# Gated stage of a fused FNet and ReGLU layer: cross parts of the fifth block in seven stacked matmuls, two products copied into further banks

## The chip, the cores and the metric

The kernel runs on one core of one Trainium2 chip. The metric is the time of one execution in microseconds, as the device measures it; times before are the median of 3 runs. Five engines work side by side, each through its own queue in order: TensorE (PE; its weight loads are shown apart as PEld), VectorE (DVE), ScalarE (ACT), GpSimd (POOL) and SyncE (SP). In this kernel SP and POOL mostly issue DMA transfers.

## The reference

```python
xn = layernorm(x)                       # x: 2048 tokens x 640
a, b = xn @ hid_re.T, xn @ hid_im.T     # 640 x 640
y = seq_re @ a - seq_im @ b             # 2048 x 2048
gate, up = xn @ W_gate, xn @ W_up       # 640 x 1728 each
h = where(gate > 0, gate, 0) * up
out = x + y + h @ W_down                # 1728 x 640
```

All of it is in fp32. This document is about the line of `gate` and `up`, and about what stands around it.

## The kernel before, in words

The layer runs in three stages. The first streams the sequence DFT in four chunks of 512 tokens (`NCHUNK`, names B11, B21, T1, T2, B22, T3, T4) and leaves its products in DRAM. The second, the gated stage, computes gate and up. The third multiplies by the hidden DFT and by W_down and adds everything up.

TensorE is used with fp32r operands. To keep fp32 accuracy each operand is split into a high part (rounded to fp32r by ScalarE) and a low part (the rest, by VectorE): `split`, L124 and L125. A product is then three matmuls, `mm3`, L130 to L132: high by high, high by low, low by high.

The gated stage works feature-major. The 640 features are five blocks of 128, the 1728 columns of the weights are 13 blocks of 128 (`NF`) and a rest of 64. Two halves of the tokens (`q` = 1, then 0) of 1024 tokens each give 26 units (`NU`), one call of `gate_up(n)` each; `gate_up_rest` does the 64 columns before the first and after the last unit. A unit computes gate and up for 128 columns and two chunks of 512 tokens. Seen as 2 x 2 blocks (gate and up by the two chunks) the first four feature blocks are multiplied in seven block products in place of eight, after Strassen and Winograd: the weights' sums S1 to S4 and the data's sums T1 to T4 stand beside the plain blocks A11, A12, A22 and B11, B21, B22. The fifth feature block is not part of this scheme; it is multiplied by itself in `block4` (A4 for gate, U4 for up, G4 their difference; data X4).

TensorE writes into PSUM banks of 128 x 512. In a unit the order on TensorE is: A11 into b1, A12 and A4 into b2, S1 and U4 into b4, S2 onto b1, A22 and U4 into b3, G4 and S4 onto b4, S3 onto b1. Between two products onto the same bank, ScalarE copies the bank out: `p1`, `ob`, `u2`, `u3` (`copy`, L121). VectorE adds the parts (`oa`, L907 and L935). `finals` (L871 to L873) of a unit is written into the next unit, after its first product.

The weights of a unit are prepared one unit ahead (class `Weights`): the DMA into `z` on SP (L840), four sums and G4 on VectorE (`sums`, L846 to L850), rounding on ScalarE (`high`), low parts on VectorE (`low`, L860), into one of two tiles `gw`. In unit 0 this stands later in the unit than in the others, since the weights of unit 1 land late.

Further work is hung into the units by lists: `issues` and `urgent` after `finals`, `loads` with the weights ahead, `besides` after the bank b3 has been given its work. It is: the data sets of the other half of the tokens (`token_step` and `token_sets`, units 1 to 9; they leave whole sets in DRAM), loading and splitting them (`next_set`, units 9 to 13 and 24), and the weights of the third stage (`pair_weights`, L1018 to L1021 and L125, one in each of units 13 to 24; `keep` stores it one unit later). PE, DVE, ACT and POOL keep the order in which the code is written (`manual_schedule`); SP's order is made by a planner.

SBUF is given out by pools; the pools of the gated stage take the place of those of the streaming stage, and a transfer into a new tile waits for the users of the old tiles there. `stage` is a pool of two tiles that lives through both.

Of the kernel before, what the change touches and what calls it, by code (L numbers as in the profile page):

```python
# [7 lines left out]
F32 = mybir.dt.float32  # L8
# [4 lines left out]
P = 128  # L13
S, D, F = 2048, 640, 1728
KD = D // P
CH = 512
# [25 lines left out]
A11, A12, A22 = (2 * P * i for i in range(3))  # L42
A4, U4, G4 = (6 * P + P * i for i in range(3))
S1, S2, S3, S4 = (9 * P + 2 * P * i for i in range(4))
NZ = 17 * P
NRAW = 10 * P
# [12 lines left out]
def fnet_reglu_kernel(  # L59
# [25 lines left out]
    get_gw0 = lambda: gw0_p.tile([P, 2, NZ], F32R, name="gw")  # L85
# [10 lines left out]
    halves = dram_p.tile([NSET, P, 2, W2], F32, name="set1")  # L96

# [263 lines left out]
    def token_sets(q, step, place=None, unit=None):  # L361
# [15 lines left out]
        if step < 2:  # L377
# [12 lines left out]
            made = [([make], "a", lambda v: halves[X4][:, v, cs], lambda ap: ap)]  # L390
            keep_whole = lambda: nc.gpsimd.dma_start(sets[X4][:, cs], t["a"])
# [36 lines left out]
        if unit:  # L428
            unit(load, made[0][0], keep_whole)
            return  # L430

        def halve(name):
            src = t[name]
            t["h" + name] = h = work()[:, : src.shape[1]]
            split(h.bitcast(F32R), src.bitcast(F32R), src)

# [6 lines left out]
        return load, made[0][0], halves_of  # L443

# [9 lines left out]
    def s4_part(g):  # L454

        if "s4" not in late:
            late["s4"] = get_gw0().rearrange("p v z -> p (v z)")
# [314 lines left out]

    early_sets, first_sets = list(SETS_A), list(SETS_B)
# [9 lines left out]
    for step in range(2, SET_STEPS):  # L783
# [6 lines left out]
        at(c, "B22", 2 * i + 1, *([halve["mr"]] if i else halve.values()))  # L790

    def phase(c, names):


        for n in names.split():
            if n == "K":
# [19 lines left out]
    phase(NCHUNK - 1, "T10 T11 T12 T13 T20 B220 T21 B221 T22 T23 K K K A A B222 B223 T30 A T31 A T32 A T33 T40 T41 T42 T43 K")  # L816
# [7 lines left out]
    for n, b, side in (("prep", 2, "left"), ("tmp", 1, "left"), ("wr", 1, "left"), ("hob", 2, "left"), ("z", 2, "left"),  # L824
                       ("stage3", 2, "left"), ("sets", 1, "left"), ("gw1", 1, "right")):
        open_pools[n] = ph2.enter_context(tc.tile_pool(name=n, bufs=b, side=side, reuse_waits="tile"))
    pool = open_pools.__getitem__
    stage3 = lambda: pool("stage3").tile([P, W2], F32, name="st")
    get_gw = (get_gw0, lambda: pool("gw1").tile([P, 2, NZ], F32R, name="gw"))
    NU = 2 * NF  # L830
    tt = nc.vector.tensor_tensor
    SUMS = 8 * P

    class Weights:


        def __init__(self, n):
            self.z2 = pool("z").tile([P, 2 * P + NZ], F32, name="z")
            with tc.issue_after(late["dma"]):
                self.ins = nc.sync.dma_start(self.z2[:, :NRAW], wgu[n % NF]).ins  # L840
            self.n, self.z = n, self.z2[:, 2 * P :]

        def sums(self):
            a21, z = self.z2[:, : 2 * P], self.z
            zz = lambda b: z[:, b : b + 2 * P]
# [540 lines left out]
```

## Time and profile before

| | |
|---|---|
| median of 3 runs | 1025.42 us (1024.63 to 1025.64) |
| span of the profiled execution | 1023.0 us; the page gives no time beside it, and the median stands 2.4 above |
| TensorE busy | 1019.0 us, 4524 matmuls |
| VectorE, ScalarE, GpSimd busy | 816.7, 435.0, 123.1 us |
| granted TensorE clock | 1.000 |
| gated units | 404.1 to 722.4 us |

Busy shares are means over the three stages. A row of a view reads: source line, engine, operation, tile written <- tiles read, shape, count, then busy time and mean duration. In a view in order of time a row begins with start and duration in us, and what stands in brackets at its end is the engine's idle time ahead of it and who ended it. Consecutive instructions of an engine overlap a little in these rows.

### The profile page before, as it was taken

The page shows a single profiled execution, that of the slowest core. Times are in us where ns is not written, and L with a number is a line of the kernel's source. Part 1 is how long each engine was busy: PE and PEld are TensorE (multiplying, and loading weights), DVE is VectorE, ACT ScalarE, POOL GpSimd, SP SyncE. Part 2 cuts the span into 40 slices and gives each one's busy share as a digit, 9 for nine tenths or more (in the row PEclk, how much of TensorE's full clock was granted, in tenths as well). Part 3 has the DMA queues.
Part 4 walks back from the last instruction along what each step waited for, and adds up shares of the span by engine and source line. Part 5 has one row for each costly group of instructions (what it writes and reads, how often), then busy time and mean ns, then how long its engine had stood idle before and what let it go on. Part 6 is the DMA issues. An engine that isn't in the chain of part 4 may idle for free.

```text
span 1023.0 us, 12536 instructions
## 1 busy us (share of the span) xinstructions
PE 1019.0 (100%) x4524; PEld 844.3 (83%) x4524; DVE 816.7 (80%) x1102; ACT 435.0 (43%) x554; POOL 123.1 (12%) x193
## 2 busy tenths in 40 slices
PE   9999999999999999999999999999999999999998
PEld 8888888888888888888888888888888888888887
DVE  7957977998989576788878988888686895777983
ACT  5654453443433333433335444444544434544442
POOL 3521001012210001112210000011100000000000
PEclk9999999999999999999999999999999999999999
DMA  8897734958969885555547676674999467896624
GB/s 321 310 299 284 257 127 160 339 196 272 359 235 350 304 320 148 187 191 180 178 145 271 217 251 239 237 271 166 326 399 307 126 237 252 281 322 214 225 95 139
DMA packets 91389, 249.12 MB, mean 244 GB/s; under 512 B 11328, under 2 KB 32384, under 8 KB 88640
## 3 DMA queue, kind: packets, MB, share of 16 engines
q1 hardware_dynamic: 72720, 174.11, 49.8%
q0 software_dynamic: 18176, 73.67, 19.8%
q8 instruction: 35, 0.57, 0.2%
q10 hardware_dynamic: 432, 0.56, 0.1%
q14 instruction: 26, 0.21, 0.1%
HBM read 185.63 MB, written 61.62 MB: 242 GB/s over the span
## 4 chain that ended last, share of the span: by engine, by line
PE 100%; ACT 0%; issue 0%
PE ps L132 31%; PE ps L131 31%; PE ps L130 31%; PE ps L511 3%; PE ps L541 1%; PE ps L1233 1%; PE ps L112 0%; PE ps L1238 0%; PE ps L1248 0%; ACT y L121 0%
## 5 line engine op out<-in xcount | busy, mean ns | idle before, releaser
L124 ACT ACTIVATE cb<-rw 128x1024 fp32r<-128x1024 f32 x83 | 81.6, 988 | 135.1 <-PE ps L132 96.8
L125 DVE TENSOR_TENSOR cb<-rw,cb 128x1024 fp32r<-128x1024 f32 x83 | 93.7, 1131 | 48.3 <-ACT cb L124 48.1
L124 ACT ACTIVATE cb<-raw 128x1024 fp32r<-128x1024 f32 x71 | 75.3, 1060 | 114.5 <-PE ps L132 106.3
L125 DVE TENSOR_TENSOR cb<-raw,cb 128x1024 fp32r<-128x1024 f32 x71 | 86.8, 1223 | 40.3 <-ACT cb L124 39.9
L130 PE MATMUL ps<-cb,wt 128*128 128x512 f32 x270 | 105.0, 389 | 0.0
L131 PE MATMUL ps<-cb,wt 128*128 128x512 f32 x270 | 105.0, 389 | 0.0
L132 PE MATMUL ps<-cb,wt 128*128 128x512 f32 x270 | 105.0, 389 | 0.0
L130 PE MATMUL ps<-xs_early,gw 128*128 128x512 f32 x260 | 101.2, 389 | 0.0
L132 PE MATMUL ps<-xs_early,gw 128*128 128x512 f32 x260 | 101.1, 389 | 0.0
L131 PE MATMUL ps<-xs_early,gw 128*128 128x512 f32 x260 | 101.1, 389 | 0.0
L121 ACT ACTIVATE gw<-z 128x1024 fp32r<-128x1024 f32 (+1 forms) x52 | 57.7, 1110 | 79.3 <-DVE z L850 78.4
L130 PE MATMUL ps<-cb,xs_late 128*128 128x512 f32 x232 | 90.2, 389 | 0.0
L131 PE MATMUL ps<-cb,xs_late 128*128 128x512 f32 x232 | 90.2, 389 | 0.0
L132 PE MATMUL ps<-cb,xs_late 128*128 128x512 f32 x232 | 90.2, 389 | 0.0
L130 PE MATMUL ps<-cb,xs_early 128*128 128x512 f32 x226 | 87.9, 389 | 0.0
L131 PE MATMUL ps<-cb,xs_early 128*128 128x512 f32 x226 | 87.9, 389 | 0.0
L132 PE MATMUL ps<-cb,xs_early 128*128 128x512 f32 x226 | 87.9, 389 | 0.0
L121 ACT ACTIVATE u<-ps 128x512 f32<-128x512 f32 x52 | 31.2, 599 | 89.1 <-PE ps L132 89.1
L860 DVE TENSOR_TENSOR gw<-z,gw 128x1024 fp32r<-128x1024 f32 (+1 forms) x52 | 64.7, 1283 | 1.3 <-ACT gw L121 1.2
L130 PEld LDWEIGHTS ps<-cb,wt 128*128 128x128 f32 x270 | 50.7, 188 | 10.6
L131 PEld LDWEIGHTS ps<-cb,wt 128*128 128x128 f32 x270 | 50.7, 188 | 10.6
L132 PEld LDWEIGHTS ps<-cb,wt 128*128 128x128 f32 x270 | 50.7, 188 | 10.4
(195 smaller groups left out, 2210.1 us busy)
## 6 DMA issues: line engine op xcount, KB each, us to landing
raw<-in_dft SPq DMA_DIRECT2D x94, 512.0 KB, 5.9
z<-in_wgu SPq DMA_DIRECT2D x26, 640.0 KB, 4.5
wd<-wparts SPq DMA_DIRECT2D x30, 512.0 KB, 5.7
wparts<-pw POOLq DMA_DIRECT2D x12, 1152.0 KB, 5.3
hd<-ob POOLq DMA_DIRECT2D x26, 512.0 KB, 2.9
rw<-hd SPq DMA_DIRECT2D x24, 512.0 KB, 7.1
tk<-in_dft SPq DMA_DIRECT2D x16, 512.0 KB, 6.0
set<-r POOLq DMA_DIRECT2D x16, 512.0 KB, 4.2
```

The lines of the kernel that those rows point to most:

```text
L121: return nc.scalar.activation(o, i, AF.Copy)
L124: nc.scalar.activation(hi, src, AF.Copy)
L125: return nc.vector.tensor_tensor(lo, src, hi.bitcast(F32), op=OP.subtract)
L130: nc.tensor.matmul(ps, wh, mh, start=first, stop=False, skip_group_check=more)
L131: nc.tensor.matmul(ps, wh, ml, start=False, stop=False, skip_group_check=more)
L132: nc.tensor.matmul(ps, wl, mh, start=False, stop=last, skip_group_check=more)
L511: start["pe"] = pin([nc.tensor.matmul(E[0, key], xn_part(n * SG + j, d)[v == 1], b[:, int(v == 2), j], start=False, stop=n % NH == NH - 1 ...
L541: pin([nc.tensor.matmul(E[c, key], xn_part(j, d)[v == 1], b[c][0][:, int(v == 2), j], start=j == 0 and v == 0, stop=False)])
L860: tt(self.w[:, 1, cs], self.z[:, cs], self.w[:, 0, cs].bitcast(F32), op=OP.subtract)
L1233: nc.tensor.matmul(B[out], w[:, 0, v, oo : oo + P], b[:, 0, 0], start=False, stop=last and v == 1, skip_group_check=more)
```

## The change

For the fifth block, the two cross parts (high by low and low by high) leave `block4` and enter the seven-product scheme. The block's 128 rows are cut in two halves of 64, which take the place of a row more in the 2 x 2 scheme. For one half, the weights' high part (64 rows) and low part (64 rows) are stacked into one 128-row operand, and against it stand the data's low and high part stacked; so one matmul adds both cross parts. Each of the seven products gets one such matmul (`product`: six and one), and what remains of `block4` is one matmul, high by high (`fifth_product`), four times in a unit.

The host lays the weights out with the half blocks twice (`twice`), so a unit's weights are 14 x 128 columns in place of 10. On the chip the lower 64 rows of them become low parts (`fifth_high` on ScalarE, `fifth_low` on VectorE), the sums S1 to S4 are made over three blocks each, and only the main two blocks of each get a low part. The data's seven stacks are made once for each half of the tokens (`cross_sets`, four subtractions), kept in DRAM (`crossed`) and loaded into SBUF in three pieces a, b, c (`load_cross`).

The order on TensorE is now: A11 into b1, S1 into b4, S2 onto b1, A12 and A4 onto c, S3 onto b1, S4 and A4 onto b4, U4 onto d, A22 and U4 onto b1. ScalarE copies b1 after A11 into bank c, and b4 after S1 into bank d; TensorE adds onto these copies. Gate's first part leaves c through a Relu on ScalarE.

The diff, cut to its core:

```diff
-A11, A12, A22 = (2 * P * i for i in range(3))
...
+S1, S2, S3, S4 = range(4)
+A11, A12, A22 = range(4, 7)
+P3 = 3 * P
+HS, HA, A4, U4, LOWS = 0, 12 * P, 21 * P, 22 * P, 23 * P
...
+    def cross_sets(q, place):
...
+        def load():
+            t["s"], t["t"] = place(), place()
+            for i, r in enumerate((lo, hi)):
+                for rows, v in ((lo, 1), (hi, 0)):
+                    nc.gpsimd.dma_start(t["s"][rows, i * W2 : (i + 1) * W2], fifth[q][r, v])
...
+        return load, [sub(t1, b12, b11), sub(t2, b22, t1), sub(t3, b22, b12), sub(t4, b21, t2)], keep
...
+    CROSS_PLACES = {"a": (XB11, 2), "b": (XT2, 2), "c": (XT3, 3)}
...
+    def load_cross(q, name):
+        i, n = CROSS_PLACES[name]
+        t = open_pools["cx"].tile([P, 3 * CH], F32R, name="cx") if name == "c" else stages[-1].tile([P, W2], F32R, name="st")
...
+        return nc.sync.dma_start(t[:, : n * CH].bitcast(F32), crossed[q][:, i * CH : (i + n) * CH])
...
+    load, subs, keep = cross_sets(1, work_pair)
+    at(NCHUNK - 2, "T4", 2, load)
+    for g, sub in enumerate(subs):
+        at(NCHUNK - 1, "T1", g, sub)
+    at(NCHUNK - 1, "T2", 0, keep)
...
         if unit:
-            unit(load, made[0][0], keep_whole)
+            unit(load, made[0][0] if step > 1 else [lambda: (make(), halve("a"))], keep_whole)
             return
...
+        def fifth_high(self):
...
+            copy(self.rounded, self.own)
+        def fifth_low(self):
+            tt(self.own, self.own, self.rounded.bitcast(F32), op=OP.subtract)
         def sums(self):
...
+            tt(s1, a21, a22, op=OP.add)
+            tt(s2, s1, a11, op=OP.subtract)
+            tt(s3, a11, a21, op=OP.subtract)
+            tt(s4, a12, s2, op=OP.subtract)
+        def high_sums(self, i):
+            cs = slice(i * 2 * P3, (i + 1) * 2 * P3)
+            copy(self.w[:, cs], self.s[:, cs])
+        def high_own(self):
+            copy(self.w[:, HA:LOWS], self.z[:, P3:])
...
     def finals(n):
-        tt(ob[:, c1], ob[:, c1], u3, op=OP.add)
-        tt(ob[:, c0], b3, u3, op=OP.add)
-        nc.vector.scalar_tensor_tensor(ob, oa, 0.0, ob, op0=OP.max, op1=OP.mult)
+        tt(ob[:, c1], d, u3, op=OP.add)
+        nc.vector.scalar_tensor_tensor(ob[:, c1], oa, 0.0, ob[:, c1], op0=OP.max, op1=OP.mult)
+        tt(ob[:, c0], ob[:, c0], b1, op=OP.mult)
```

`gate_up` after the change, from its first product on:

```python
        if ahead and n:
            ahead.fifth_high()
        product(b1, A11, B11, XB11, True, True)
        if n > 0:
            finals(n - 1)
        for f in issues[n]: f()
        for f in urgent[n]: f()
        copy(c, b1)
        if ahead and n:
            ahead.fifth_low()
            ahead.sums()
        product(b4, S1, T1, XT1, True, True)
        copy(d, b4)
        if n == NF - 1:
            load_cross(0, "a")
        product(b1, S2, T2, XT2, last=True)
        if ahead and n:
            ahead.high_sums(0)
        copy(u2, b1)
        product(c, A12, B21, XB21)
        fifth_product(c, A4, 0)
        nc.scalar.activation(ob[:, c0], c, AF.Relu)
        if n == NF - 1:
            load_cross(0, "b")
        def rest_ahead():
            if ahead:
                ahead.high_sums(1); ahead.low_sums(); ahead.high_own()
            for f in loads[n]: f()
        if n:
            rest_ahead()
        product(b1, S3, T3, XT3, last=True)
        copy(u3, b1)
        if ahead and n:
            ahead.low_own()
        product(b4, S4, B22, XB22)
        fifth_product(b4, A4, 1)
        tt(oa, b4, u2, op=OP.add)
        if ahead and not n:
            ahead.fifth_high(); ahead.fifth_low(); ahead.sums(); ahead.high_sums(0)
            rest_ahead()
            ahead.low_own()
        for f in besides[n]: f()
        fifth_product(d, U4, 1)
        product(b1, A22, T4, XT4)
        fifth_product(b1, U4, 0)
        if n == NF - 1:
            load_cross(0, "c")
        held[n] = b1, d, u3, oa, ob
```

Before unit 0, SP loads in the written order the weights of unit 0, the rest's weights, the stacks c and b, and the weights of unit 1; the stack a is loaded at the end of the streaming stage (`load_first_cross`). The stacks of the other half are made in unit 10 (`cross_step`). The sets that `next_set` loads now come straight into their place and are split there, and X4 needs no split any more.

226 lines of the change are left out of this document (132 added, 94 removed).

## The prediction, made before the changed kernel was run

> **What bounds the kernel now.** First the page (span, busy shares, slices, the chain that ended last) and the clock.
>
> ```profile
> span 1023.0 us, 12536 instructions
> PE 1019.0 (100%) x4524; PEld 844.3 (83%) x4524; DVE 816.7 (80%) x1102; ACT 435.0 (43%) x554; POOL 123.1 (12%) x193
> ...
> PE   9999999999999999999999999999999999999998
> ...
> PE 100%; ACT 0%; issue 0%
> ...
> core 0: 1023.0 us, clock 1.000
> PE ps L112 <- PEq L1379: 0.8, 1, 0.8
> ```
>
> TensorE is the chain, from first to last, at full granted clock, and its only wait in the whole trace is 0.8 us before the first matmul. So a matmul removed is time removed, and a wait added to TensorE is time added in full; nothing covers it. The span is 1023.0; the median of the runs is 1025.42, so 2.4 us lie around the profiled span, and I add my sum to 1025.42.
>
> Then the groups by form and the order of time in the gated stage. There every matmul has the same shape.
>
> ```profile
> L130 PE MATMUL ps<-xs_early,gw 128*128 128x512 f32 x260 | 101.2, 389 | 0.0
> L130 PE MATMUL ps<-r,gw 128*128 128x512 f32 x104 | 40.5, 389 | 0.0
> L130 PE MATMUL ps<-sets_b,gw 128*128 128x512 f32 x104 | 40.5, 389 | 0.0
> ...
> 587.75 0.39 PE L130 MATMUL ps<-xs_early,gw 128*128 128x512 f32 x1
> ...
> 588.88 0.39 PE L132 MATMUL ps<-xs_early,gw 128*128 128x512 f32 x1
> ...
> 599.99 0.39 PE L130 MATMUL ps<-xs_early,gw 128*128 128x512 f32 x1
> ```
>
> Each of L130, L131 and L132 has 260 + 104 + 104 = 468 of them: 1404, or 54 in each of 26 units. Unit 15 starts at 587.75 and unit 16 at 599.99: 12.24 us for 54, 0.22667 us each. Times inside a unit below count from its first matmul.
>
> **Gain.** Before, a unit has seven blocks of six matmuls and four fifth blocks of three: 54. After, it has seven products of seven (six and one cross matmul) and four single fifth products: 53. 26 units save 26 x 0.22667 = 5.89 us. All else that I find costs.
>
> **What the other engines must do in time.** The work of VectorE and ScalarE in unit 15, in order of time:
>
> ```profile
> 588.64 0.69 DVE L871 TENSOR_TENSOR ob<-ob,u 128x512 f32<-128x512 f32 x1 [1.10 <-ACT u L121]
> 589.25 0.69 DVE L872 TENSOR_TENSOR ob<-ps,u 128x512 f32<-128x512 f32 x1
> 589.97 1.23 DVE L873 SCALAR_TENSOR_TENSOR ob<-oa,ob 128x1024 f32<-128x1024 f32 x1
> ...
> 595.78 0.42 DVE L1018 TENSOR_TENSOR pw<-pw 128x256 f32<-128x256 f32 x1
> 596.23 0.42 DVE L1019 TENSOR_TENSOR pw<-pw 128x256 f32<-128x256 f32 x1
> 596.58 0.42 DVE L1020 TENSOR_TENSOR pw<-pw 128x256 f32<-128x256 f32 x1
> 596.91 0.42 DVE L1021 TENSOR_TENSOR pw<-pw 128x256 f32<-128x256 f32 x1
> 597.91 0.96 DVE L125 TENSOR_TENSOR pw<-pw 128x768 f32<-128x768 f32 x1 [0.58 <-ACT pw L124]
> 598.83 0.69 DVE L935 TENSOR_TENSOR oa<-ps,u 128x512 f32<-128x512 f32 x1
> ...
> 588.01 0.60 ACT L121 ACTIVATE u<-ps 128x512 f32<-128x512 f32 x1 [2.06 <-PE ps L132]
> 588.50 1.05 ACT L121 ACTIVATE gw<-z 128x1024 fp32r<-128x1024 f32 x1
> 589.45 0.59 ACT L121 ACTIVATE p<-ps 128x512 f32<-128x512 f32 x1
> 592.90 1.17 ACT L121 ACTIVATE gw<-z 128x1152 fp32r<-128x1152 f32 x1 [2.85 <-DVE z L850]
> ```
>
> Both follow the written order of the code, one after another. From these rows: VectorE starts an instruction 0.08 before the end of the one ahead (588.64, 0.69 long, then 589.25), and 0.03 after it where it needs its result (589.25 to 589.97); ScalarE starts 0.10 before the end (588.01, 588.50). The p copy at 589.45 begins 0.57 after the start of the last matmul that it needs (588.88). L935 ends a line of VectorE work without a break from 588.64, but for 0.58 waiting on ScalarE: in this unit VectorE is done at 11.8 of 12.24. The rows for the new shapes:
>
> ```profile
> L125 DVE TENSOR_TENSOR wt<-wr,wt 128x384 fp32r<-128x384 f32 x12 | 6.6, 550 | 0.0
> L554 DVE SCALAR_TENSOR_TENSOR sb<-sb,sa 128x512 f32<-128x512 f32 x8 | 5.5, 682 | 0.0
> 403.54 0.67 DVE L964 TENSOR_TENSOR st<-ps,st 64x512 f32<-64x512 f32 x1
> L124 ACT ACTIVATE wt<-wr 128x768 fp32r<-128x768 f32 x39 | 32.5, 834 | 12.3 <-DMA wr<-wparts 7.7 <-PE ps L132 2.0 <-DMA wr<-in_hid 1.3
> 1016.08 0.37 ACT L121 ACTIVATE ps<-ps 128x256 f32<-128x256 f32 x1 [4.38 <-PE ps L132]
> L963 ACT ACTIVATE st<-ps x4: 596/596/597, 402.3 to 729.4; 64x512 f32<-64x512 f32 x4
> L130 PEld LDWEIGHTS ps<-sets_b,gw 128*128 128x128 f32 x104 | 19.5, 188 | 4.0
> ```
>
> A sum of 384 columns is 0.55, a multiply of 512 with a maximum 0.68, a subtraction on 64 partitions by 512 0.67, a rounding of 768 columns 0.84. A copy from bank to bank is 0.37 for 256 columns, so I take a 512-column one, and the Relu from a bank (L963), at 0.60, like the copies of before. It could be 0.1 more or less; the sums below shift by that once for each waiting unit.
>
> Now the slack. Before, the second product's copy (u2) had 18 matmuls, 4.1 us, between S2 and S3, which writes the same bank; 18 also stood between A11 and S2 for p. After, only A12 and one fifth product, eight matmuls or 1.8 us, stand between S2 and S3. And ahead of that copy ScalarE must now round the sums S1 and S2 of the next unit's weights (before it rounded raw weights there, which waited for no VectorE work), which VectorE makes behind finals and behind the extra work (besides) of the unit before. That work stood ahead of the last addition of a unit; now it stands behind it, while VectorE idles in mid-unit for the third and fourth sums to be rounded. So a ring closes from S3 of one unit to S3 of the next:
>
> S3's first matmul 0; last of S4 and its fifth 14 x 0.22667 = 3.17 later, addition 0.50 after that: 3.67; next instruction 4.28. The pair weights of units 13 to 24 (L1018 to L1021, ScalarE's rounding, the 0.96 subtraction) take 3.05 from L1018 to L935: 7.33. Finals, three of 512 columns, 0.72 + 0.61 + 0.61: 9.27. The fifth's low part, whose result the sums need, 0.72: 9.99. S1 0.59, S2 0.55: 11.13. Rounding of both from 11.17, next start 0.74 later: 11.91. The u2 copy 0.60: 12.51. Then TensorE.
>
> What TensorE loses from the end of that copy to the matmul has no row, as it never waited. Lower end 0.04, the hand-over between VectorE and ScalarE (597.91 begins 0.03 after the rounding); upper end 0.30, that plus the weight load that then stands free (0.19) and 0.07. I take 0.17, nearer the weight load. The ring is 12.68, against 53 x 0.22667 = 12.01 for the matmuls: 0.67 of wait in each of units 14 to 24, eleven units, 7.4 us.
>
> **Unit 1.** Its weights are now made in unit 0 wholly behind the addition of S4's bank, and A11, its first product, needs the two parts written last.
>
> ```profile
> 407.80 0.69 DVE L907 TENSOR_TENSOR oa<-ps,p 128x512 f32<-128x512 f32 x1 [2.16 <-PE ps L132]
> ...
> 412.72 0.43 DVE L846 TENSOR_TENSOR z<-z 128x256 f32<-128x256 f32 x1 [4.23 <-DMA z<-in_wgu]
> ...
> SPq L840 <- DMA pq<-sa: 16.3, 1, 16.3
> ...
> z<-in_wgu SPq DMA_DIRECT2D x26, 640.0 KB, 4.5
> ```
>
> Unit 0 began at 404.13. After: addition at 404.13 + 43 x 0.22667 + 0.50 = 414.38 (0.50 as at L907: 15th matmul 407.30, L907 407.80). Fifth's low part 414.99; sums 415.71, 416.29, 416.76, 417.23, end 417.78. Third and fourth sum rounded from 417.82; 1152 columns of own weights 418.56 to 419.73 (1.17 as at 592.90); the low part of the sums holds VectorE until 419.84, own low part until 420.79. Unit 1 was due at 416.15 and its third matmul at 416.60; with 0.17 it starts that one at 420.96: 4.36 us. Before, these sums began at 412.72, when the weights had landed, ahead of that addition.
>
> The clock was 1.000 through the whole trace, with TensorE never idle; by that the sum has nothing for restarting. [...]
>
> **Units 2, 13 and the odd ones.** In unit 1 the fifth block's halves are now made on the spot, twice (0.72 + 0.73 for the products, rounding 0.64, subtraction 0.61 = 2.7, 5.4 in all) where 2.7 stood: the ring is 12.68 - 3.05 + 5.4 = 15.0, and unit 2 waits 3.06 (1.64 of it already before S2, whose copy c stands behind those roundings). At unit 12 four splits of 1024 stand behind the addition, and one more ahead of the sums in unit 13; two of them before:
>
> ```profile
> 561.93 2.35 DVE L125 TENSOR_TENSOR xs_early<-pw,xs_early 128x1024 fp32r<-128x1024 f32 x2
> ```
>
> Five at (2.35 - 0.08) / 2 = 1.14 are 5.7: ring 15.3, wait 3.3 in unit 13, of which 2.35 at A11, which needs the third split (B11). In units 3, 5, 7, 9 and 11 the 2.7 us of token or cross work of the unit before give a ring of 12.3: 0.26, three times 0.33, 0.21, together 1.5.
>
> Laid out in the same way, the units of before never make TensorE wait, and VectorE is done in unit 15 at 11.8, as its rows show; so the rules of thumb hold there.
>
> **Sum.** -5.9 + 4.4 + 3.1 + 3.3 + 1.5 + 7.4 = +13.8 us with the hand-over at 0.17. It is paid in some 19 waits; at 0.04 the sum is 2.5 less, +11.3, at 0.30 it is +16.3.
>
> **Taken at nothing.** Four subtractions of 0.69 in the last chunk's streaming:
>
> ```profile
> 325.00:345.00 20.00, 20.00 (x90) 16.54 (x89) 14.64 (x14) 5.97 (x7) 0.92 (x2) 1.00 0.92 332
> ```
>
> VectorE is busy 14.64 of 20 there, so 2.8 us fit; without that cover they would cost up to 2.8. Their stores and the load behind the K loads go to queues that run four units ahead. The weights grow from 640 to 896 KB a unit; 640 KB landed in 4.5 us (the row of z above, its median), and they are loaded a unit ahead. In unit 12 the loads of the next half's stacks wait on SP for S1, A12 and A22, with the first pair weights and unit 15's weights behind them; each is due more than 8 us after it can go. POOL's added stores wait for work of the unit before, done by then. The first unit's weights need about as much VectorE time as before. The loads of the stacks b and c before unit 0 I also set at nothing, with one doubt priced below. In the last stage nothing changes.
>
> **Rivals.**
> (a) The order is not as written: VectorE takes the sums into its mid-unit idle time and unit 1's weights ahead of the addition. Its place is the position of the besides work; the ring opens, and TensorE loses nothing: 1025.42 - 5.9 = 1019.5, faster. It decides if the ring is under 12.01, that is if 0.67 of the 3.05 leave it. Against it: every row of unit 15 stands in written order. 0.10.
> (b) Rings all fit, unit 1's wait stays: -5.9 + 4.4 = 1023.9, no difference. The same 0.67, and 3 us in units 2 and 13, would have to come from shorter hand-overs. 0.07.
> (c) The rings of 12.3 and 12.7 fit, units 1, 2 and 13 wait: -5.9 + 4.4 + 3.1 + 3.3 = +4.9, 1030.3. It decides at 0.05 less on each of the fourteen links; the overlaps of 0.08 and 0.10 bear that much error. 0.09.
> (d) Stacks late: the load of c takes memory that before held sa, as the weights of unit 1 did before: the queue waited 16.3 us for the store of sa, and those 640 KB had landed only at 412.7 (L846). c, 768 KB, is due at 412.1 in S3: at worst 1 us late. b is due at 404.13 + 20 x 0.22667 = 408.7 in S2; if it queues behind c it lands no earlier than 412.7: +4, 1043.2. For it speaks the order of the code; against it, that a load whose place is free may go ahead. 0.08.
> (e) TensorE comes back slow from the 3.75 us without a matmul in unit 1: eight matmuls at twice 0.22667 add 1.8: 1041.0. No row shows TensorE idle, so none speaks for it or against; the other waits are shorter. 0.03.
> That the change saves no matmuls is excluded by the count.
>
> **Numbers.** My forecast, the waits of all rings, has the remaining 0.63; its time is 1025.42 + 13.8 = 1039.2, its own range 1036.7 to 1041.7 by the hand-over. With (c), (d) and (e) the range is 1028 to 1045; (a), (b) and some 0.03 above stay out. A difference of 0.2% (2.05 us) is about what can be told here: faster 0.10 (a), same 0.07 (b), slower 0.83.
>
> **What would show it.** 1378 gated matmuls; TensorE idle some 20 us between 404 and 735, led by the u2 copy of ScalarE ahead of S3; 0.7 in each of units 14 to 24; about 4 at unit 1's A11 for own weights, 3 in units 2 and 13. VectorE idle in mid-unit, then busy past the unit's end. Were L1018's work back ahead of the addition, or TensorE without waits, I am wrong at the ring; were the u2 copy long done when S3 starts, at its terms.

## The result, and the profile after

The changed kernel takes 1062.76 us (median, 1060.54 to 1063.45) against 1025.14 for the kernel before beside it: 1.0362 times as long, 95% interval 1.0348 to 1.0377. The forecast was 1039.2, at most 1045. The direction was right and the time 23.6 us short.

First the page of the profile after: span, busy shares, the slices of TensorE and of its granted clock, and the chain that ended last.

```profile
span 1060.4 us, 12554 instructions
PE 1028.3 (97%) x4498; PEld 843.0 (80%) x4498; DVE 812.5 (77%) x1085; ACT 484.2 (46%) x633; POOL 135.4 (13%) x215
...
PE   9999999999969999799999999999799999999998
...
PEclk9999999999989999999999999999999999999999
...
PE 72%; issue 15%; DVE 6%; ACT 3%; DMA 2%; POOL 1%; SPq 0%; POOLq 0%; DVEq 0%; ACTq 0%
```

26 matmuls fewer, as counted. But TensorE's line has three dents, near 310, 430 and 750 us: the gated stage lies between 415 and 751, so the first and the last are outside the stage that the change names. The waits of TensorE put names to them (total, times, longest):

```profile
PE ps L137 <- DVE cb L131: 8.3, 1, 8.3
PE ps L136 <- ACT u L127: 6.4, 15, 1.1
PE ps L136 <- ACT wt L130: 5.7, 1, 5.7
PE ps L136 <- ACT gw L127: 3.8, 1, 3.8
PE ps L136 <- ACT ps L127: 1.5, 1, 1.5
PE ps L137 <- DVE xs_early L131: 1.2, 1, 1.2
...
PE ps L136 <- ACT xs_early L130: 0.6, 1, 0.6
PE ps L138 <- DVE gw L935: 0.3, 1, 0.3
```

`gw`, `u`, `ps` and `xs_early` are the waits of the gated stage that the prediction has. The 8.3 us for `cb` (a streamed operand) and the 5.7 us for `wt` (a weight of the third stage) are not in it. The windows (us, busy time and count for PE, PEld, DVE, ACT and POOL, then granted clock, DMA share, GB/s) show something besides waiting:

```profile
300.00:325.00 25.00, 16.69 (x65) 13.28 (x64) 12.37 (x16) 4.90 (x5) 5.35 (x9) 0.80 0.63 220
...
576.00:592.00 16.00, 14.26 (x55) 10.98 (x54) 13.57 (x18) 11.53 (x15) 0.53 (x1) 0.89 1.01 372
...
605.00:745.00 140.00, 135.23 (x583) 108.39 (x583) 107.70 (x173) 76.83 (x111) 11.98 (x25) 1.00 0.64 243
745.00:775.00 30.00, 24.27 (x95) 19.28 (x94) 13.25 (x16) 10.78 (x15) 4.31 (x8) 0.89 0.74 257
```

In the windows that hold the two long waits and unit 13 the mean granted clock is 0.80 and 0.89. Before, it was 1.000 throughout.

Since TensorE is the chain, the time can be put into places from its matmuls alone: the distance from one start to the next, less 0.22667, is time lost. Before, that sums to 0.23 us after the first fifty matmuls; after, to 43.3. With the 26 matmuls (5.9) taken off that is 37.2 more, and the spans, 1060.4 and 1023.0, differ by 37.4. By place, here and in every kernel run below (us; each from one profiled execution):

| kernel | streaming | unit 1 | unit 2 | units 3 to 11, odd | unit 13 | units 14 to 24 | entry of third stage | all | median | ratio, 95% interval |
|---|---|---|---|---|---|---|---|---|---|---|
| predicted | 0 | 4.4 | 3.1 | 1.5 | 3.3 | 7.4 | 0 | 19.7 | 1039.2 | |
| after | 10.7 | 6.3 | 3.3 | 2.1 | 4.0 | 8.0 | 8.8 | 43.3 | 1062.76 | 1.0348 to 1.0377 |
| e1_ring | 11.5 | 6.7 | 3.2 | 0.0 | 4.3 | 7.5 | 8.4 | 41.9 | 1061.13 | 1.0331 to 1.0367 |
| e2_unit0 | 9.6 | 0.0 | 3.2 | 2.1 | 3.5 | 7.9 | 8.7 | 35.2 | 1054.85 | 1.0277 to 1.0308 |
| e3_stream | 11.2 | 5.9 | 3.3 | 2.2 | 4.5 | 7.9 | 8.2 | 43.4 | 1062.72 | 1.0360 to 1.0394 |
| e8_stream2 | 9.0 | 6.5 | 3.3 | 2.2 | 3.9 | 8.0 | 8.8 | 41.9 | 1060.07 | 1.0320 to 1.0357 |
| e10_stream3 | 0.2 | 6.0 | 3.3 | 2.1 | 3.9 | 8.0 | 8.6 | 32.3 | 1051.09 | 1.0246 to 1.0274 |
| e4_entry | 8.8 | 6.0 | 3.3 | 2.1 | 3.9 | 8.0 | 5.8 | 38.1 | 1058.57 | 1.0318 to 1.0353 |
| e7_entry2 | 11.9 | 6.7 | 3.3 | 2.2 | 3.9 | 8.0 | 5.6 | 41.8 | 1060.10 | 1.0327 to 1.0360 |
| e11_entry3 | 10.9 | 6.6 | 3.3 | 2.2 | 3.9 | 8.0 | 0.0 | 35.1 | 1053.79 | 1.0264 to 1.0295 |
| e9_best | 7.2 | 0.0 | 0.0 | 0.0 | 0.5 | 0.0 | 5.9 | 14.2 | 1035.28 | 1.0081 to 1.0113 |
| e12_best2 | 0.2 | 0.0 | 0.0 | 0.0 | 0.5 | 0.0 | 0.0 | 1.3 | 1020.74 | 0.9948 to 0.9973 |

One of the four runs of e3_stream took 2096.33 us and is left out of its median. In e9_best and e12_best2 the sum holds another 0.4 us lost in unit 12. The streaming stage is the same in the changed kernel, e1_ring, e2_unit0, e4_entry, e7_entry2 and e11_entry3, and it lost 8.8 to 11.9 us there; so up to 3 us between two executions can come from it alone, and each edit is judged by its own place.

The gated stage lost 23.7 us where 19.7 was forecast. The other 19.4 us were lost in two places that the prediction had "taken at nothing". The theory tested below: three separate causes, each of which can be removed by itself (the order of work in the gated stage; four subtractions that stop VectorE in streaming; memory layout at the third stage's entry). The rivals: that streaming and entry are late because of the added traffic, or because of the gated stage's own delay.

### The profile page after: what moved, and what is told of

Read it like the earlier page. It is cut to its first block, busy times and chain, and to the rows that moved or that the text cites. A ratio compares the mean times of both kernels' runs of the same rounds, so it can differ in the third digit from the quotient of the medians.

```text
span 1060.4 us, 12554 instructions
## 1 busy us (share of the span) xinstructions
PE 1028.3 (97%) x4498; PEld 843.0 (80%) x4498; DVE 812.5 (77%) x1085; ACT 484.2 (46%) x633; POOL 135.4 (13%) x215
## 4 chain that ended last, share of the span: by engine, by line
PE 72%; issue 15%; DVE 6%; ACT 3%; DMA 2%; POOL 1%; SPq 0%; POOLq 0%; DVEq 0%; ACTq 0%
PE ps L136 22%; PE ps L137 22%; PE ps L138 22%; PE ps L545 3%; ACT gw L127 2%; PE ps L965 1%; DMA wparts<-pw 1%; PE ps L575 1%; DVE gw L935 1%; PE ps L968 1%; PE ps L1352 1%; DVE z L915 1%; POOL set L448 1%; DVE ob L954 1%; DVE sets_b L416 0%
## 5 line engine op out<-in xcount | busy, mean ns | idle before, releaser
L131 DVE TENSOR_TENSOR cb<-rw,cb 128x1024 fp32r<-128x1024 f32 x83 | 93.8, 1132 | 47.8 <-ACT cb L130 46.1
L131 DVE TENSOR_TENSOR cb<-raw,cb 128x1024 fp32r<-128x1024 f32 x71 | 86.8, 1223 | 37.6 <-ACT cb L130 37.2
L136 PE MATMUL ps<-cb,wt 128*128 128x512 f32 x270 | 106.3, 394 | 5.7 <-ACT wt L130 5.7
L138 PE MATMUL ps<-cb,wt 128*128 128x512 f32 x270 | 106.1, 393 | 0.0
L137 PE MATMUL ps<-cb,wt 128*128 128x512 f32 x270 | 106.0, 393 | 0.0
L935 DVE TENSOR_TENSOR gw<-zs,gw 128x1024 fp32r<-128x1024 f32 x26 | 31.9, 1226 | 52.8 <-ACT gw L127 52.7
L127 ACT ACTIVATE gw<-z 64x512 fp32r<-64x512 f32 (+1 forms) x52 | 52.2, 1003 | 30.5 <-PE ps L968 24.3
L136 PE MATMUL ps<-xs_early,gw 128*128 128x512 f32 x156 | 61.4, 394 | 4.4 <-ACT gw L127 3.8
L137 PE MATMUL ps<-xs_early,gw 128*128 128x512 f32 x156 | 61.3, 393 | 1.2 <-DVE xs_early L131 1.2
L138 PE MATMUL ps<-xs_early,gw 128*128 128x512 f32 x156 | 61.5, 394 | 0.3 <-DVE gw L935 0.3
L127 ACT ACTIVATE gw<-zs 128x768 fp32r<-128x768 f32 x52 | 43.9, 845 | 37.6 <-DVE zs L922 37.5
L138 PEld LDWEIGHTS ps<-cb,wt 128*128 128x128 f32 x270 | 51.2, 190 | 11.2 <-DVE wt L131 0.5
L137 PEld LDWEIGHTS ps<-cb,wt 128*128 128x128 f32 x270 | 51.4, 190 | 10.6
```

Of the source, the lines that this page charges most:

```text
L127: return nc.scalar.activation(o, i, AF.Copy)
L131: return nc.vector.tensor_tensor(lo, src, hi.bitcast(F32), op=OP.subtract)
L136: nc.tensor.matmul(ps, wh, mh, start=first, stop=False, skip_group_check=more)
L137: nc.tensor.matmul(ps, wh, ml, start=False, stop=False, skip_group_check=more)
L138: nc.tensor.matmul(ps, wl, mh, start=False, stop=last, skip_group_check=more)
L935: tt(self.w[:, o : o + n * 2 * P].rearrange("p (k n) -> p k n", k=n), main(src), main(self.w[:, at : at + n * P3]).bitcast(F32), op=OP.sub ...
```

## The gated stage: ring and first units

The ring in unit 16, in order of time (after):

```profile
616.66 0.56 DVE L922 TENSOR_TENSOR zs<-zs,z 128x384 f32<-128x384 f32 x1
...
617.31 0.85 ACT L127 ACTIVATE gw<-zs 128x768 fp32r<-128x768 f32 x1 [1.83 <-DVE zs L922]
...
617.88 0.39 PE L968 MATMUL ps<-xs_early,gw 128*128 128x512 f32 x1
618.06 0.58 ACT L127 ACTIVATE u<-ps 128x512 f32<-128x512 f32 x1
...
618.69 0.50 PE L136 MATMUL ps<-sets_b,gw 128*128 128x512 f32 x1 [0.43 <-ACT u L127]
...
619.03 0.39 PE L137 MATMUL ps<-sets_b,gw 128*128 128x512 f32 x1
```

ScalarE waits for VectorE's second sum (L922), rounds S1 and S2, and only then comes the u2 copy, for which TensorE stands at S3. The copy ends at 618.64; S3's first matmul is recorded at 618.69 and the second 0.34 later in place of 0.227, so the hand-over costs 0.05 + 0.11 = 0.16 (0.17 had been taken). Each of units 15 to 24 loses 0.72 in this way (unit 14: 0.82); units follow at 12.73 (ring as worked out: 12.68).

The ring was opened by taking the work beside the products (`besides`) off its place behind the last addition:

```diff
+        ahead_of = n not in (1, 11, 12, 24)
+        if ahead_of:
+            for f in besides[n]:
+                f()
         nc.scalar.activation(ob[:, c0], c, AF.Relu)
...
-        for f in besides[n]:
-            f()
+        if not ahead_of:
+            for f in besides[n]:
+                f()
```

> The changed kernel with besides moved ahead of the Relu of bank c in all units but 1, 11, 12 and 24, nothing else. Theory of the ring (VectorE reaches the sums late because the extra work stands behind the last addition): the waits at S3 in units 3, 5, 7, 9, 11 and 14 to 24 go, 0.70 each in the eleven last and 0.3 to 0.5 in the others, 9.5 us together; perhaps 1 us comes back as a wait of A22 in unit 13: 1053 to 1054.5. Rival (ScalarE, with five bank copies and Relu a unit, is itself too late, wherever the extra work stands): the waits stay, 1062 to 1063.

Measured: every one of the sixteen short waits of units 3 to 11 and 14 to 24 is gone, which is what the ring's theory says. The median fell by 1.6 us only, to 1061.13, since one new loss of 7.5 us came in, at 656.2 (e1_ring, its waits of TensorE over the span, then those of the stretch 640 to 660 for VectorE and SP's queue):

```profile
PE ps L136 <- ACT u L127: 8.0, 4, 5.5
```

```profile
DVE pw L1135 <- DMA pw<-in_wd: 7.0, 1, 7.0
```

```profile
SPq L1130 <- DMA wparts<-pw: 17.2, 2, 11.4
```

The pair weights are now wanted some 8 us earlier in the unit (first sum 3.7 us after the unit's start in place of 11.5), but their load stands at the place of the pair before last until that pair's store (`keep`, still issued a unit later) has landed. In the other units that is in time; here the store issued at 636.19 took 10.6 us to land, its neighbours 5.0 to 8.4. Opening a ring at one link brings forward the due time of everything on it.

Unit 1, in order of time (after); unit 0 began at 414.86:

```profile
425.10 0.69 DVE L1018 TENSOR_TENSOR oa<-ps,u 128x512 f32<-128x512 f32 x1 [8.73 <-PE ps L968]
...
430.81 0.96 DVE L935 TENSOR_TENSOR gw<-z,gw 128x768 fp32r<-128x768 f32 x1
430.83 0.50 PE L136 MATMUL ps<-xs_early,gw 128*128 128x512 f32 x1 [3.80 <-ACT gw L127]
...
431.82 0.64 PE L138 MATMUL ps<-xs_early,gw 128*128 128x512 f32 x1 [0.26 <-DVE gw L935]
432.25 0.63 PE L136 MATMUL ps<-xs_early,gw 128*128 128x512 f32 x1
432.68 0.63 PE L137 MATMUL ps<-xs_early,gw 128*128 128x512 f32 x1
```

The addition comes 10.24 into unit 0 (10.25 worked out), the third matmul of unit 1 at 16.96 (16.83). VectorE stood idle for 8.73 ahead of the addition: the weights of unit 1 could have been made there. And from 431.82 on the matmuls are 0.43 apart in place of 0.227, eight of them in this unit; the granted clock is 0.5 from 432.04 to 435.46.

```diff
-        if ahead and n:
+        if ahead:
...
-        if ahead and not n:
-            ahead.fifth_high()
...
-            ahead.low_own()
```

> The changed kernel with unit 0 preparing unit 1's weights at the place where the other units prepare theirs. Theory (the chain behind unit 0's last addition keeps A11 of unit 1 waiting; the weights have landed long before): the 4.5 us of waits at A11 of unit 1 go, and with them the matmuls at half the rate behind them (about 1.5 us): 1056 to 1057.5. Rival (unit 1's weights or the tile that they go to are what is late): the wait only moves, into unit 0 or to A11 of unit 1, and the time is within 1.5 us of 1062.8.

Measured: unit 1's 6.3 us are gone, 1054.85 us in place of 1062.76; no other place moved by more than about 1 us. The time lies 1 us below the theory's range; the streaming stage, which the edit does not touch, lost 1.1 less in the profiled execution. Rival (d) of the prediction (stacks landing late in unit 0) does not come up: unit 0 has no wait in either kernel.

## The streaming stage: three tries

VectorE, POOL and TensorE about 300 us, in order of time (after):

```profile
299.21 1.22 DVE L711 TENSOR_TENSOR raw<-tk,raw 128x1024 f32<-128x1024 f32 x1
...
303.05 0.77 POOL L448 DMA_DIRECT2D set<-r  x1 [4.45 <-issue]
...
307.33 0.76 POOL L448 DMA_DIRECT2D set<-r  x1 [3.50 <-issue]
308.08 0.55 POOL L463 DMA_DIRECT2D r<-set  x1
...
313.06 0.69 DVE L470 TENSOR_TENSOR r<-r 128x512 fp32r<-128x512 f32 x1 [12.63 <-DMA r<-set]
...
314.94 0.80 PE L137 MATMUL ps<-cb,gw 128*128 128x512 f32 x1 [8.31 <-DVE cb L131]
```

The first cross subtraction (L470) held VectorE for 12.6 us. It waited for its source, whose fourth load (L463) stood on POOL behind stores of the token steps (L448). These go out 4 to 5 us apart, each some 0.3 us after the landing of the one ahead (landings at 302.69 and 307.02). Behind it in VectorE's order stood the low part (L131) that TensorE needed. First try: the loads on another queue.

```diff
-                    nc.gpsimd.dma_start(t["s"][rows, ...], fifth[q][r, v])
+                    (nc.sync if q else nc.gpsimd).dma_start(t["s"][rows, ...], fifth[q][r, v])
```

> The changed kernel with the four loads of the fifth block's half blocks in the streaming stage issued by SyncE in place of GpSimd. Theory (the fourth load stands in GpSimd's queue behind three stores, VectorE's first subtraction waits 12.6 us for it and holds the low parts that TensorE needs): TensorE's 8.5 us wait at 306 goes, and with it the nine matmuls at half the rate: 1051.5 to 1053. Rival (the place or the data of that load is late, not the queue): the wait stays or moves to SyncE's loads of the DFT matrix, 1060 or more.

Measured: the rival's outcome; the wait stays (11.2 us) under another name (e3_stream, waits of VectorE and of SP's queue, 285 to 325):

```profile
DVE r L470 <- DMA set<-r: 12.7, 2, 9.9
```

```profile
SPq L463 <- DMA set<-r: 12.5, 2, 9.4
```

It is now the stores themselves: the cross parts use four of the eight places of the token steps' work region, and stores from those places are still out. Second try: the places whose stores go out first.

```diff
-        i = (late["places"] + 2) // 2 * 2 % 8
-        late["places"] = i + 1
+        i = late["places"] = 2 if late["places"] == 5 else 6
```

> The changed kernel with the four loads of the cross parts' source on SyncE, and with their place moved to the two places of the work region whose stores go out first (the rounded halves of step 4; the destination of the subtractions in the places of step 4 itself) instead of step 4 and step 5. Theory (the wait in streaming was for places whose stores were still out, and VectorE carried it to TensorE): of the 10.7 us of excess at 306 at most 2 is left; 1052 to 1054.5 us. Rival (the loads themselves are late beside the streamed ones, or VectorE has no room for four more subtractions): 6 us or more is left, 1058 us or more.

Measured: 1060.07 us, the rival's number, but not by its cause. The wait is 9.0 us at 296.6. In the order of time (e8_stream2):

```profile
300.40 0.69 DVE L470 TENSOR_TENSOR r<-r 128x512 fp32r<-128x512 f32 x1 [11.06 <-DMA set<-r]
```

The subtraction ran 13 us earlier than in the changed kernel and still 11 us late: VectorE reaches it at 289 now, not at 300, for it also stands further forward in VectorE's order. The loads were not late: the last landed at 296.88, and the subtraction began when a store (L448) landed, at 300.37. (That VectorE keeps the written order holds for the gated stage alone; in streaming a planner makes its order too.) The planner put the subtraction ahead of the landing of the store that held its place; why it moved it forward stays open. Third try: hold the four subtractions behind the low parts of two later units.

```diff
-    at(NCHUNK - 2, "T4", 2, load)
-    for g, sub in enumerate(subs):
-        at(NCHUNK - 1, "T1", g, sub)
-    at(NCHUNK - 1, "T2", 0, keep)
...
+    def behind_lows(sub):
+        def run():
+            with tc.issue_after(lows[-1].ins):
+                sub()
+        return run
...
+    at(NCHUNK - 2, "B22", 3, load)
+    for i, sub in enumerate(subs):
+        at(NCHUNK - 2, "T3", i // 2, behind_lows(sub))
+    at(NCHUNK - 2, "T3", 2, keep)
```

> The changed kernel with the loads and places of the last streaming run, and with the four cross subtractions held behind the rounding subtractions of the units T3 0 and T3 1 of the third chunk: some three streamed units (10 us) later in VectorE's order, at about 305 and 308 instead of 300. Theory (VectorE works in order, and the planner puts the subtractions ahead of the landing of the store that held their place, 300.4 in the last run; whatever stands behind them waits, TensorE with it): of the 10.6 us of excess in streaming at most 1 is left, 1051 to 1053.5 us. Rival (the stores of the cross parts or the loads on SyncE take the time from the streamed transfers wherever they stand): 5 us or more is left, 1057 us or more.

Measured: 1051.09 us; 0.2 us is left in streaming. The subtractions (e10_stream3, in order of time) start without a wait:

```profile
305.11 0.68 DVE L470 TENSOR_TENSOR r<-r 128x512 fp32r<-128x512 f32 x1
...
306.85 0.68 DVE L470 TENSOR_TENSOR r<-r 128x512 fp32r<-128x512 f32 x1
...
308.59 1.28 DVE L470 TENSOR_TENSOR r<-r 128x512 fp32r<-128x512 f32 x2
```

The same loads, stores and subtractions are in it, so traffic and VectorE's time are not the cause. The loads and the stores (`keep`) were given other places in the code as well, but the loads go out at 282.53 to 291.14, in e8_stream2 at 282.68 to 291.76; so what differs from that run is above all the place of the subtractions. That this alone, without the other queue and the other places in memory, would do was not tried.

## The entry of the third stage: two locks on memory

SP's queue at the entry (after, waits from 745 to 775):

```profile
SPq L1244 <- PE ps L138: 20.9, 1, 20.9
SPq L1244 <- DVE gw L131: 7.2, 1, 7.2
SPq L1244 <- PE ps L1357: 3.7, 1, 3.7
...
```

The second raw load of the third stage (L1244) waited for the last matmuls that read `gw`; SP's loads from the second on came at 761.98 and after, 11 us behind the end of the last unit, where the kernel before had them at 722.59 and after, right as its last unit ended. In the memory layout of the two programs, the grown tile of stacked weights reaches down to 168960 (170496 before), and the fourth group of raw tiles of the third stage goes up to 169728: now they overlap by 768 bytes. Two kernels test this from both sides. The first gives only the layout to the kernel before:

```diff
-    ... lambda: pool("gw1").tile([P, 2, NZ], F32R, name="gw"))
+    ... lambda: pool("gw1").tile([P, 37 * P], F32R, name="gw")[:, : 2 * NZ].rearrange(...))
```

> The kernel before, with the tile of the stacked weights of odd units 1536 bytes longer per partition than it uses (37 blocks of 128 columns in place of 34); not one instruction is added or removed. Its lower end then lies where it lies in the changed kernel, at 168960, and the last 768 bytes of the fourth group of raw tiles of the third stage (145152 to 169728) overlap it. Theory (a lock on memory at the entry of the third stage, set by layout alone): the second raw load of the third stage goes out only after the last matmuls that read this tile, and TensorE waits 6 to 9 us at the entry, so 1031 to 1034 us. Rival (the entry's wait comes from the later gated stage or from what the change added to the queues): 1025 us, no wait at the entry.

Measured: 1033.23 us against 1024.82, ratio 1.0079 (1.0063 to 1.0095); TensorE loses 7.9 us at 733.6 and, after the first fifty matmuls, nowhere else. The instructions are the same ones; the planner has ScalarE and VectorE take some of them at and behind the entry in another order. Its SP queue and TensorE, 725 to 775:

```profile
...
SPq L1125 <- DVE gw L125: 6.8, 1, 6.8
SPq L1125 <- PE ps L1238: 3.8, 1, 3.8
```

```profile
PE ps L130 <- ACT wt L124: 5.4, 1, 5.4
```

The second takes the overlap from the changed kernel:

```diff
-    ... *((f"raws{i}", 6, "left") for i in range(4)), ...
+    ... *((f"raws{i}", 6, "left") for i in (1, 2, 3, 0)), ...
```

> The changed kernel with the pools of the third stage's loads laid out in another order (1, 2, 3, 0), so that the pool whose end lies over the gated stage's second weight tile is the one that is loaded last. Theory (that tile is 1536 bytes longer than before, a load tile of the third stage now lies over its first 768 bytes, so the second load waits for the lead products that read it, and SyncE's queue behind it): the 6 us wait at the entry of the third stage goes with the ten matmuls at half the rate behind it, 1053.5 to 1055. Rival (the entry waits for the rest's result or its store, which moved into the tile of the data sets): no difference, 1062 to 1063.5.

Measured: 1058.57 us, between theory and rival. SP's loads run from 748.8, yet 5.8 of 8.8 us stay. ScalarE (e4_entry, in order of time) has a new holder:

```profile
756.57 1.05 ACT L130 ACTIVATE cb<-rw 128x1024 fp32r<-128x1024 f32 x1
763.13 0.84 ACT L130 ACTIVATE wt<-wr 128x768 fp32r<-128x768 f32 x1 [5.52 <-issue]
```

The profile names no holder. Its loads had landed; the store to `hrest` (L1074), which the rival names, landed at 763.06, right ahead of the 763.13 of the row. The change had moved its source into the free region (`late_place(3)`, `late_place(4)`), under the first split weights of the third stage. Place 4 overlaps them by bytes, so the places were changed:

```diff
-        rg, hh = (late_place(i) for i in (3, 4)) if n else ...
+        rg, hh = (late_place(i) for i in (2, 3)) if n else ...
```

> The changed kernel with the raw tiles of the third stage laid out in the order 1, 2, 3, 0 (as in the run before of this kind) and the two tiles of the rest (the Relu and the product that is stored to hrest) in places 2 and 3 of the free region instead of 3 and 4; place 4 overlapped the first tile of the split weights of the third stage by 2560 bytes, places 2 and 3 lie under the third and fourth tile of the data ring. Theory (two locks in series, nothing else): of the 8.9 us of excess at the entry at most 1 is left; 1053.5 to 1055 us. Rival (a third holder behind them, the weight load or the store of the last unit): 4.5 us or more is left, 1058 us or more.

Measured: no gain; 5.6 us stay, and the same wait of ScalarE: 766.23, 5.28 of idle time, with the store issued at 761.02 and landed at 766.16. It is no third holder. The lock is on the whole tile of eight places, of which the first split weights overlap some (the kernel opens its pools with `reuse_waits="tile"`). So the store's source was put outside that tile:

```diff
-        rg, hh = (late_place(i) for i in (3, 4)) if n else ...
+        rg, hh = (pool("z").tile([P, NRAW], F32, name="z")[:, :W2] for _ in range(2)) if n else ...
```

> The changed kernel with the raw tiles of the third stage in the order 1, 2, 3, 0 and the two tiles of the rest in a pool of their own (the two raw weight tiles, free by then) instead of the free region. In the last two entry runs ScalarE's first weight split of the third stage waited for the store to hrest, also where that store read a place that the split's tile did not overlap: so the wait is for the whole tile of eight places, which the split's tile does overlap. Theory (the lock holds per tile, not per place): with the store's source outside that tile the entry keeps at most 1 us of its 8.7; 1053.5 to 1055 us. Rival (that ScalarE waits for the store itself or the weight load behind it, wherever its source lies): 5 us or more is left, 1058 us or more.

Measured: 1053.79 us, nothing lost at the entry (TensorE's waits, 725 to 775, the whole list):

```profile
PE ps L136 <- ACT u L127: 0.4, 1, 0.4
```

Here the same store lands at 766.13, and ScalarE's first weight split begins at 760.41: it does not wait for the store itself.

So the entry is two locks in series, both of layout, and neither has to do with how late the gated stage is.

## All cures together

Apart from what was shown: work beside the products ahead of the Relu of bank c, with the pairs' stores issued at once; token steps 0 and 1 in units 1 and 2; the splits for the second half spread over units 11 to 13; pairs in units 14 to 24. First with the second streaming try and the places of e7_entry2:

```diff
+        for f in amid[n]:
+            f()
         nc.scalar.activation(ob[:, c0], c, AF.Relu)
...
-                besides[n + i].append(m)
+                amid[n + i].append(m)
...
-        besides[n].append(prepare)
...
-        issues[n + 1].append(keep)
+        where = besides if k == NPAIR - 1 else amid
+        where[n] += [prepare, keep]
...
-    for step, n in enumerate((1, 1, 2, 4, 6, 8)):
+    for step, n in enumerate((1, 2, 2, 4, 6, 8)):
...
-    for i, n in ((T2, 11), (T1, 11), (T4, 12), (T3, 12)):
-        next_set(i, n)
+    for i, n, where in ((T1, 11, amid), (T2, 11, besides), (T3, 11, besides), (T4, 13, amid)):
+        next_set(i, n, where=where)
...
-        pair_weights(k, 13 + k)
+        pair_weights(k, min(14 + k, 24))
```

> All cures together: unit 0 makes unit 1's weights at the usual place; work beside the products (token steps, cross subtractions, pairs) ahead of the Relu of bank c; token steps 0 and 1 in units 1 and 2; splits at unit 11 (one ahead of the Relu, two behind the addition), unit 12 (B11 ahead, B21 behind) and unit 13 (B22 with the urgent ones, T4 ahead of the Relu); pairs in units 14 to 24, two in unit 24, their stores issued at once; B12's split in unit 25; the streaming and entry changes of the two kernels above. Theory (the 26 matmuls are saved in full when nothing waits): worked through by the order on each engine with the rows' durations, the gated stage keeps 0.8 us of waits, so 5.1 us below the kernel before; with 0 to 3 us left in streaming and at the entry 1020 to 1023 us. Rival (the further copies and subtractions cannot be hidden, some wait stays in each unit): 1026 us or more.

Measured: 1035.28 us, the rival's number but not its cause: streaming kept 7.2 and the entry 5.9. The gated stage kept 0.9 us (0.8 worked out): the prediction's way of laying the units out engine by engine holds for another order too. Then with the third streaming try and the last entry edit (their diffs as above):

> The run with all cures together, with the streaming and entry changes of the two kernels above in place of the former ones. There the gated stage had kept 0.8 us of waits, streaming 7.1 and the entry 5.9. Theory (26 matmuls of 0.22667 us, 5.9 us, less 0.8 us of waits in the gated stage and at most 1 us each elsewhere): 1019.5 to 1022 us. Rival (streaming or entry keep 5 us): 1025 us or more.

Measured: 1020.74 us (1020.36 to 1021.54) against 1024.82 beside it, ratio 0.9961 (0.9948 to 0.9973): faster than the kernel before by 0.3 to 0.5%. Its page and the window of the gated stage:

```profile
span 1019.8 us, 12569 instructions
PE 1013.8 (99%) x4498; PEld 838.5 (82%) x4498; DVE 812.0 (80%) x1085; ACT 485.6 (48%) x633; POOL 132.9 (13%) x211
...
PE 99%; DMA 1%; ACT 0%; ACTq 0%; issue 0%; DVE 0%
```

```profile
404.00:722.00 318.00, 318.00 (x1401) 262.26 (x1400) 249.95 (x391) 178.82 (x253) 52.29 (x90) 1.00 0.72 257
```

TensorE is the chain again, at full clock. Of the 5.9 us of the saved matmuls 4.1 arrive in the medians. In the profiled execution, the slowest of the five, 1.1 us more than before are lost by the table (1.3 against 0.2), and 1.3 at the very start, where neither the kernel before nor the changed kernel had waited: the 61st matmul begins at 10.59, before at 9.28 (TensorE's waits over the span):

```profile
PE ps L575 <- ACT cb L331: 1.1, 1, 1.1
...
PE ps L575 <- DVE xs_early L336: 0.5, 1, 0.5
```

The first of the two is the loss; ScalarE itself waited 1.28 us there for a load (`raw`). The second cost nothing: the short matmuls on constants ahead (L118) were done earlier, and the first matmul of the work begins at 5.44, before at 5.49. The edits do not touch that place; e4_entry, e6_pad and e11_entry3 lose 0.5 us there too. What makes the load vary stays open.

## Why the prediction was right and wrong

- **Gain, 5.9:** right; 4498 matmuls, and with the waits gone it shows.
- **Ring, 7.4:** 8.0 measured, 0.72 each for 0.67. Right in mechanism and size; undoing it (e1_ring) removed those waits. The hand-over, taken at 0.17 between 0.04 and 0.30, cost 0.16 in unit 16; no row shows the 0.07 in the upper end.
- **Unit 1, 4.4:** 6.3 measured. The waits are some 4.6; the rest is eight matmuls at the slow rate, 1.6 to 1.7 (rival (e) priced eight at 1.8). One term was read wrong (the own weights' rounding takes 1408 columns and 1.38 us, not the 1152 columns and 1.17 us of the row used).
- **Units 2 and 13, 3.1 and 3.3:** 3.3 and 4.0, of which seven slow matmuls (585.74 to 588.72) are 1.4; in e2_unit0 unit 13 lost 3.5. Unit 2 was not taken apart by itself, nor was unit 13; in the last kernels unit 2 loses nothing, units 12 and 13 0.4 and 0.5.
- **Odd units, 1.5:** 2.1.
- **Rival (e), the clock, 0.03:** it happened, and not only in unit 1: 33 matmuls at 426 to 427 ns in four places, 6.6 us. The chance was the error: no row of before could speak for it, but neither against it. Its 3.75 us come from the sums of unit 1 (419.73 + 0.17 - 416.15); its eight matmuls at twice 0.22667 were the author's assumption, which no row of before shows. In their place the run showed, in unit 1, a wait of 3.80 us and eight matmuls at 1.88 times 0.22667. Behind the waits of 5.7 and 8.3 us stood ten and nine, behind the waits of units 2 to 11 and 14 to 24, with up to 1.7 us lost, none. Unit 13's two waits close together, 0.7 and 1.5 us lost, were followed by seven (the last section has the figures).
- **"Taken at nothing", streaming:** the step that failed, 10.7 us. The prediction priced the subtractions' time (2.8 us on a VectorE with room) and not their operands: the load behind POOL's stores, the places behind the same stores. The sentence on queues "that run four units ahead" spoke of the cross parts' own stores and loads and missed that L463 is issued on POOL behind stores it had not placed in time. The runs showed in its place: L470 held VectorE for 12.6 us until its source and its place were free, and TensorE lost 8.3 us waiting for the low part behind it and 2.4 more mostly to nine slow matmuls; with the subtractions further back 0.2 is left. What stood behind L470 in VectorE's order paid that wait, on an engine that in the kernel before was busy 14.64 of 20 us in that stage (325 to 345).
- **"In the last stage nothing changes":** the other step that failed, 8.8 us. Its instructions did not change; the memory it takes over did. The kernel's description names the rule (a transfer into a new tile waits for the users of the old tiles there), and the prediction applied it to the stack c in rival (d), but not to the two tiles that the change made longer or moved. The runs showed in its place two locks in series: 768 bytes of overlap alone cost 7.9 us (e6_pad), and with both taken away 0.0 is left (e11_entry3).
- **The range** had its upper end at 1045 from rivals inside the gated stage only. Both failed steps lay outside that stage and had no rival; they make 19.4 of the 23.6 us.

## What to carry to other kernels

When a change makes a tile longer or moves one, go through what later takes those addresses, up to the next stage: 768 bytes of overlap cost 7.9 us with not one instruction changed. Price an added instruction on an in-order engine by when its operands and its place are ready, not by how long it runs or how idle the engine is on average: L470 runs 0.69 us and held VectorE for 12.6. When a ring is closed by work at one link, moving that work opens it, but the loads and stores feeding the work must be moved too: in e1_ring the sixteen short waits went and 7.5 us came in at a load.

## What the runs showed of the hardware

- Behind its three long waits in the changed kernel TensorE's matmuls started 426 to 427 ns apart in place of 226.67 (1.88 times, at a granted clock of 0.5): nine behind the 8.3 us, eight behind the 3.8, ten behind the 5.7, so 1.6 to 2.0 us on top of each. In e6_pad they started 0.43 us apart as well, behind its wait of 5.4 us (740.99, 741.42, 741.85).
- In the changed kernel the granted clock is 0.5 from 309.16 to 319.40, 432.04 to 435.46, 585.64 to 589.06 and 766.55 to 773.38. By the trace's record these are 10.240, 3.413, 3.413 and 6.827 us, that is three, one, one and two times 3.413, and the stretches at full clock between them, 112.64, 150.19 and 177.49 us, are 33, 44 and 52 times 3.413. Cut into such steps, after the first fifty matmuls, eight steps at full clock lost 1.0 us or more (start to start of the matmuls, less 0.22667): the four with 2.28 to 3.41 were followed by a step at 0.5, the four with 1.01 to 1.76 by a step at full clock.
- So what a short wait cost there went with where it fell. Unit 13's two waits (0.72 and 1.45 us lost) fell into one step, 2.28 us of it lost, with seven slow matmuls behind it. Unit 2's two (1.67 and 1.28) spread over three steps, none with more than 1.39 lost, and no slow matmul followed.
- In unit 16 of the changed kernel a hand-over from a ScalarE copy to a waiting TensorE cost 0.16 us, seen as 0.05 ahead of the first matmul and 0.11 behind it.
